# Attention with two routed layers: scaling q on ScalarE for every pair of heads, and one gate transpose a step

## The chip, the cores and the metric

The kernel runs on one core of a Trainium2 chip. A core has five engines that run their own instruction streams and wait for each other by semaphores: TensorE (PE, with its weight loads PEld), VectorE (DVE), ScalarE (ACT), GpSimd (POOL) and SyncE (SP), which in this kernel issues nearly all DMA transfers. The metric is the device time of one execution in microseconds (us); lower is better. Three runs of the kernel before took 1119.1 to 1124.27 us, with a median of 1122.33 us.

## The reference

Three parts run one after the other. Only the first and the entry of the second matter here.

```python
scores = scale * q @ k.T                      # 2 x 8 heads, 576 tokens, head size 64
bias = -(cum[:, :, :, None] - cum[:, :, None, :])          # cum: running sum of max(s, 0)
scores = where(causal, -1e9, scores + minimum(bias, 0))
attn = softmax(scores);  x = attn @ v         # x: 1152 tokens x 512
logits = x @ w_gate;  noisy = logits + log1p(exp(x @ w_noise)) * noise
top2 = the two largest of 8 experts per token # first routed layer (1024 hidden) ...
# ... then a second layer in which every expert sees every token, balanced 8 times
```

## The kernel before, in words

The 16 heads are taken in 8 pairs. Every number is carried as two halves of 16 bits (a high part and the rest), so that TensorE's products stay exact enough.

**Preparing a pair** (`nat_a`, `nat_d`, L130 to L149). q and k of a pair arrive as 32-bit tiles `stq` and `stk`. ScalarE writes 32*q as the high half (L135). Then q is scaled in place in 32 bits: by ScalarE for pairs 0 to 2 (L137), by GpSimd for pairs 3 to 7 (L139). ScalarE writes the high half of k (L140). At last VectorE forms the rest of k (L146) and GpSimd the rest of q (L148), which reads the scaled tile. `turn` (L189) turns the whole with a DMA transpose.

**Steps.** A loop over `it` from -4 to 16 is a software pipeline; I call its rounds step -4 to step 16. In step i TensorE makes the transposed scores of head i (L258, L260, L263), then the plain scores of head i+3 for their row maxima (L212, L215), a small turn of the maxima of the head before (L243), and the product with v of head i-1 (L350 to L354). ScalarE exponentiates (L267, L268), VectorE takes the maxima (L226), forms the rests `el` (L271), the negated maxima (L233, L235), and copies the operands of a later head (L203, L205). From step 13 on there are no plain scores, since no head is left. The maxima go by ScalarE (`rt`, L245) and a small DMA on SP (L246) into the rows 67 and 68 of `xq`; the product L260 of that head, two steps later, needs them.

**Beside the steps.** `between(it)` at the end of a step adds other work: from step 8 to 15 it writes 640 KB of zeros into the rows of one expert in memory (`xs_d<-z`, L661); from step 12 to 15 it loads one 512 KB piece of weights (`wst`, L536); in steps 13 and 14 it turns rows of `xall` (L703); and from step 9 on it advances the generator `route` for the first 512 tokens by one `yield` a step. In this order: weights, zeros, turns, route. The next pairs of heads are loaded after it (`stv`, L104, L106).

**route, first four tiles** (`pe` false). Four DMA transposes of the attention's output (L749, 256 KB each), then the gate's products on TensorE (L689, 48 of them), then logits `lg` on VectorE (L763), `na`, `ez`, `lu` on ScalarE (L767 to L771), some small VectorE and GpSimd work, and the choice of two experts. What set the order is the place of the `yield`s: each engine executes its instructions in the order in which the program was written, and SP's transfers all go through one queue (q1 of the page).

Of the kernel before, what the change touches and what calls it, by code (L numbers as in the profile page):

```python
# [12 lines left out]
AF = mybir.ActivationFunctionType  # L13
OP = mybir.AluOpType
# [3 lines left out]
def attention(tc, ctx, psum, q, k, v, s, xhl, scat, between, idle):  # L18
    nc = tc.nc
    B, H, S, D = q.shape  # L20
    G = B * H
    SQ = 32.0
# [26 lines left out]
    for i in range(NS):  # L49
        t = cst.tile([128, 2, 5, D], F32, name=f"stv{i}")  # L50
# [3 lines left out]
    for i in range(NX):  # L54
        t = cst.tile([128, 640], F16, name=f"xk{i}")
        xk.append(t)
        t = cst.tile([128, 640], F16, name=f"xq{i}")
        xq.append(t)
    for i in range(4):
        t = cst.tile([128, 2, 5, 130], F16, name=f"vx{i}")  # L60
        vxt.append(t)
    for i in range(3):
        t = cst.tile([128, 5], F32, name=f"mx{i}")
        mx.append(t)
        t = cst.tile([128, 10], F16, name=f"rn{i}")
        rn.append(t)
    for i in range(2):
        t = [cst.tile([128, 1664], F16, name=f"e{x}{i}") for x in "hl"]
# [58 lines left out]
    def nat(p):  # L127
        nat_a(p)
        nat_d(p)

    def nat_a(p):
        np_ = wk.tile([128, 2, 9, 128], F16, name="np_", bufs=3)
        nq, nk = np_[:, 0], np_[:, 1]
        qs, ks = ld.pop(("q", p)), ld.pop(("k", p))
        nc.scalar.activation(out=nq[:, :, 64:128], in_=qs, func=AF.Copy, scale=SQ)  # L135
        if p < 3:
            nc.scalar.activation(out=qs, in_=qs, func=AF.Copy, scale=SQ)  # L137
        else:
            nc.gpsimd.tensor_scalar(out=qs, in0=qs, scalar1=SQ, scalar2=None, op0=OP.mult)  # L139
        nc.scalar.activation(out=nk[:, :, 0:64], in_=ks, func=AF.Copy, scale=SQ)  # L140
        ld[p] = np_, qs, ks

# [273 lines left out]
    for it in range(-4, G + 1):  # L416
        p = (it + 5) // 2
# [46 lines left out]
def attention_moe_moe_kernel(  # L464
# [16 lines left out]
    nc = tc.nc  # L481
# [23 lines left out]
    def bank():  # L505
        return psum.tile([128, 512], F32, name="ps", tag="b")
# [162 lines left out]
    def xhl(t, n=None):  # L669

        return xhl_v[:, t] if n is None else xhl_v[:, t:t + n]
# [20 lines left out]
    def keep(ps, n, w):  # L692

        for _ in range(n):
            nc.tensor.matmul(out=ps[:, 0:w.shape[1]], lhsT=w[:, 0:128], rhs=w, start=True, stop=True)

    def turn2(c):

        todo = [(x, t) for x in range(2) for t in range(T2)]
        for i in range(0, 2 * T2, 4):  # L700
            ps = bank()
            for j, (x, t) in enumerate(todo[i:i + 4]):
                nc.tensor.matmul(out=ps[:, j * 128:(j + 1) * 128], lhsT=xhl(4 + t)[:, x, c * 128:(c + 1) * 128], rhs=ident,  # L703
                                 start=True, stop=True)
            for x in range(2):
                js = [(j, t) for j, (y, t) in enumerate(todo[i:i + 4]) if y == x]
                if js:
                    o = xt2[:, js[0][1]:js[-1][1] + 1, x * KD + c, :]
                    src = ps[:, js[0][0] * 128:(js[-1][0] + 1) * 128].rearrange("p (t n) -> p t n", n=128)
                    if c == 1:  # L710
                        idle.append(lambda o=o, src=src: nc.scalar.activation(out=o, in_=src, func=AF.Copy))
                    elif c < KD - 2:
                        idle.append(lambda o=o, src=src: nc.vector.tensor_copy(out=o, in_=src))
                    elif c == KD - 2 and i:
                        idle.append(lambda o=o, src=src: nc.vector.tensor_copy(out=o, in_=src))
                    elif c == KD - 2:
                        idle.append(lambda o=o, src=src: nc.scalar.activation(out=o, in_=src, func=AF.Copy))
                    elif x:
                        nc.vector.tensor_copy(out=o, in_=src)
                    else:  # L720
                        nc.scalar.activation(out=o, in_=src, func=AF.Copy)
# [9 lines left out]
    def route(r_p, t0, t1, pe):  # L731

        T = t1 - t0
        V = nc.vector

        def tmp(nm, *shape, dt=F32):
            return (r_p if pe or nm not in ("hot", "rk") else hx_p).tile([128, T] + list(shape), dt, name=nm)

        if pe:
            turn2(KD - 1)  # L740
            ps = bank()
            keep(ps, K2, iotac)
            for t in range(T):
                gate_mm(ps, t, xt2[:, t], wg, 16, (KD - 2, KD - 1))
        else:
            xts = []
            for t in range(t0, t1):
                xt = r_p.tile([128, 2 * KD, 128], F16, name="xt", bufs=T)
                nc.sync.dma_start_transpose(out=xt, in_=xhl(t).rearrange("p a d -> p (a d)"))  # L749
                xts.append(xt)  # L750
                if t - t0 in (1, 3):
                    yield
            yield
            ps = bank()
            for t in range(T):
                gate_mm(ps, t, xts[t], wg, 16)
        yield
        pg = ps[:, 0:T * 16].rearrange("p (t e) -> p t e", e=16)
        lg = tmp("lg", 16)
        if pe:  # L760
            V.scalar_tensor_tensor(out=lg, in0=pg, scalar=1.0 / (SX * SG), in1=pl, op0=OP.mult, op1=OP.add)
        else:
            V.tensor_scalar(out=lg, in0=pg, scalar1=1.0 / (SX * SG), scalar2=None, op0=OP.mult)  # L763
        if not pe:
            yield
        na = tmp("na", E)
        nc.scalar.activation(out=na, in_=lg[:, :, E:2 * E], func=AF.Abs)  # L767
        ez = tmp("ez", E)
        nc.scalar.activation(out=ez, in_=na, func=AF.Exp, scale=-1.0)
        lu = tmp("lu", E)  # L770
        nc.scalar.activation(out=lu, in_=ez, func=AF.Ln, bias=onec)  # L771
        u = tmp("u", E)
        if pe:
            yield
        V.tensor_scalar(out=u, in0=ez, scalar1=1.0, scalar2=None, op0=OP.add)
        d = tmp("d", E)
        if pe:
            yield
        V.scalar_tensor_tensor(out=d, in0=u, scalar=1.0, in1=ez, op0=OP.subtract, op1=OP.subtract)
        if pe:  # L780
            yield
        V.reciprocal(out=u, in_=u)
        if pe:
            yield
        V.tensor_tensor(out=d, in0=d, in1=u, op=OP.mult)
        V.scalar_tensor_tensor(out=d, in0=lg[:, :, E:2 * E], scalar=0.0, in1=d, op0=OP.max, op1=OP.subtract)
        yield
        for b, op in ((d, OP.add), (noise_sb[:, t0:t1, :], OP.mult), (lg[:, :, 0:E], OP.add)):
            (V if pe else nc.gpsimd).tensor_tensor(out=lu, in0=lu, in1=b, op=op)
        if not pe:  # L790
            yield
        for t in range(T):
            V.max(out=m8[:, t0 + t], in_=lu[:, t])
        for t in range(T):
            V.max_index(out=i8[:, t0 + t], in_max=m8[:, t0 + t], in_values=lu[:, t])
        hot = tmp("hot", 2, E)
        it = iota8.unsqueeze(1).unsqueeze(1).to_broadcast([128, T, 2, E])
        V.tensor_tensor(out=hot, in0=it, in1=i8[:, t0:t1, 0:2].unsqueeze(3).to_broadcast([128, T, 2, E]), op=OP.is_equal)
        V.tensor_tensor(out=mb[:, t0:t1, :], in0=hot[:, :, 0], in1=hot[:, :, 1], op=OP.add)
        if pe:  # L800
            ps = spare[0]
            for t in range(NT):
                nc.tensor.matmul(out=ps[:, NT * E:NT * E + E], lhsT=ones, rhs=mb[:, t, :], start=(t == 0), stop=(t == NT - 1))
            yield
        else:
            yield
            ps = bank()
        pr = ps[:, 0:T * E]
        nc.tensor.matmul(out=pr, lhsT=tri, rhs=mb[:, t0:t1, :].rearrange("p t e -> p (t e)"), start=True, stop=False)
        for sh in range(1, t1):  # L810
            a, b = max(t0, sh), t1
            nc.tensor.matmul(out=ps[:, (a - t0) * E:(b - t0) * E], lhsT=ones,
                             rhs=mb[:, a - sh:b - sh, :].rearrange("p t e -> p (t e)"), start=False, stop=(sh == t1 - 1))
        rk = tmp("rk", E)
        V.tensor_tensor(out=rk, in0=pr.rearrange("p (t e) -> p t e", e=E),
                        in1=base8.unsqueeze(1).to_broadcast([128, T, E]), op=OP.add)
        V.tensor_tensor(out=hot, in0=hot, in1=rk.unsqueeze(2).to_broadcast([128, T, 2, E]), op=OP.mult)
        sl = slot[:, t0:t1, :]
        V.tensor_reduce(out=sl, in_=hot, op=OP.add, axis=AX.X)
        V.tensor_copy(out=idx[:, t0:t1, :], in_=sl)  # L820
        if pe:
            yield
# [107 lines left out]
    with ExitStack() as m1:  # L930
# [84 lines left out]
        for e in range(E):  # L1015
# [33 lines left out]
            for b, n in BL:  # L1049
# [8 lines left out]
                else:  # L1058

                    for f in range(KF):  # L1060
# [5 lines left out]
                                                   op0=OP.mult, op1=OP.add)  # L1066
# [417 lines left out]
```

## Time and profile before

| | |
|---|---|
| profiled execution, its own time | 1117.76 us |
| its span from first to last instruction | 1116.0 us |
| runs: lowest, median, highest | 1119.1, 1122.33, 1124.27 us |
| PE busy | 1072.7 us (96%) |
| DVE, ACT, POOL busy | 599.3, 496.3, 230.4 us |
| mean granted clock of TensorE | 0.974 of full |

A page of the profile gives the busy time of each engine; the timeline of an engine gives start, duration, line, operation, and, in square brackets, how long it sat idle before and what ended that. A busy TensorE is not one that does much: the same products take longer at the lower of its two clocks (1.2 and 2.4 GHz), which the column PEclk shows as 0.50.

### The profile page before, as it was taken

To read this page: it belongs to the slowest core of one execution; us is meant where nothing else is said; L and a number is where in the kernel's file an instruction comes from. 1 tells how busy PE (TensorE), PEld (TensorE's weight loads), DVE (VectorE), ACT (ScalarE), POOL (GpSimd) and SP (SyncE) were. 2 spreads that over 40 slices of the span, in tenths; PEclk is the share of its full clock that TensorE was granted. 3 is DMA by queue.
4 is the path that set the end of the run, shared out by engine and by line. 5 is a ranking of instruction groups with operands and counts; after the bars stand their busy time and mean duration, and the time that the engine had idled before them with its cause. 6 is when DMAs were issued, how large, how long until landed. Compare 5 with 4: busy or idle time off the path is not lost.

```text
span 1116.0 us, 18342 instructions
## 1 busy us (share of the span) xinstructions
PE 1072.7 (96%) x7412; PEld 662.2 (59%) x7412; DVE 599.3 (54%) x1171; ACT 496.3 (44%) x928; POOL 230.4 (21%) x296
## 2 busy tenths in 40 slices
PE   7998899999999799999999999999999999999997
PEld 3565765555555385565666565566566566566554
DVE  8998685555554577553554543543453453454231
ACT  5786685555555243443433442442443442443220
POOL 6675352000004303521201301210210210220000
PEclk7798899999999899999999999999999999999999
DMA  5768769777756710120120121121121112020001
GB/s 98 134 116 149 201 245 300 191 228 212 210 167 207 245 49 3 56 76 27 51 76 20 57 62 34 38 76 38 38 77 38 37 59 57 20 58 1 11 29 50
DMA packets 131469, 107.14 MB, mean 96 GB/s; under 512 B 71504, under 2 KB 105600, under 8 KB 131376
## 3 DMA queue, kind: packets, MB, share of 16 engines
q1 hardware_dynamic: 127040, 91.86, 30.5%
q0 software_dynamic: 4336, 14.03, 3.6%
q8 instruction: 60, 0.98, 0.4%
q14 instruction: 33, 0.27, 0.1%
HBM read 79.03 MB, written 17.56 MB: 87 GB/s over the span
## 4 chain that ended last, share of the span: by engine, by line
PE 63%; issue 15%; POOL 4%; DMA 3%; DVE 2%; ACT 1%; POOLq 0%; DVEq 0%; SPq 0%; ACTq 0%
PE ps L1304 32%; PE ps L1250 25%; PE ps L1104 3%; POOL xs_d L828 2%; POOL yg L926 1%; DMA yg<-y_d,idy 1%; POOL y_d L1068 1%; DVE wp L560 0%; PE ps L1030 0%; DMA xsT<-xs_d 0%; PE ps L1031 0%; PE ps L1032 0%; DMA xs_d<-xall,idx 0%; DMA y_d<-y 0%; ACT wp L559 0%
## 5 line engine op out<-in xcount | busy, mean ns | idle before, releaser
L1304 PE MATMUL ps<-wp,hop 128*128 128x512 f16 x1536 | 366.6, 379 | 0.3 <-PE ps L1178 0.3
L1250 PEld LDWEIGHTS <-wp 128*128 128x128 f16 x2352 | 230.1, 98 | 101.1 <-issue 1.6
L1304 PEld LDWEIGHTS <-hop 128*128 128x128 f16 x1536 | 150.2, 98 | 141.8 <-issue 0.4
L560 DVE SCALAR_TENSOR_TENSOR wp<-wst,wp 128x1024 f16<-128x1024 f32 (+1 forms) x156 | 182.1, 1187 | 78.4 <-ACT wp L559 78.3
L1250 PE MATMUL ps<-xall,wp 128*128 128x256 f16 (+1 forms) x1344 | 192.1, 286 | 0.6 <-ACT z L1264 0.6
L559 ACT ACTIVATE wp<-wst 128x1024 f16<-128x1024 f32 (+1 forms) x156 | 153.8, 1009 | 22.7 <-DMA wst<-in_moe_w_dram 20.3
L1250 PE MATMUL ps<-xT,wp 128*128 128x256 f16 (+1 forms) x1008 | 150.9, 286 | 0.2 <-DVE z L1268 0.2
L570 POOL TENSOR_TENSOR wst<-wst 128x256 f32<-128x256 f32 x28 | 21.5, 767 | 441.1 <-DVE wp L560 441.1
L1268 DVE TENSOR_TENSOR z<-ps,z 128x256 f32<-128x256 f32 (+1 forms) x56 | 25.6, 457 | 137.6 <-ACT z L1267 137.6
L1285 DVE SCALAR_TENSOR_TENSOR acc<-ps,P,acc 128x512 f32<-128x512 f32 (+1 forms) x64 | 47.5, 742 | 94.6 <-PE ps L1304 94.6
L1273 DVE TENSOR_TENSOR z<-ps,z 128x256 f32<-128x256 f32 (+1 forms) x56 | 25.6, 458 | 111.8 <-PE ps L1250 111.8
L1030 PE MATMUL ps<-xsT,wp 128*128 128x320 f16 x256 | 77.3, 302 | 2.6 <-DMA xsT<-xs_d 2.6
L1221 ACT ACTIVATE hop<-z 128x1024 f16<-128x1024 f32 x56 | 59.1, 1056 | 46.2 <-DVE z L1273 46.2
L1031 PE MATMUL ps<-xsT,wp 128*128 128x320 f16 x256 | 77.3, 302 | 0.0
L1032 PE MATMUL ps<-xsT,wp 128*128 128x320 f16 x256 | 77.2, 302 | 0.0
L1222 DVE SCALAR_TENSOR_TENSOR hop<-z,hop 128x1024 f16<-128x1024 f32 x56 | 68.1, 1216 | 11.1 <-ACT hop L1221 11.1
L1264 ACT ACTIVATE z<-ps 128x256 f32<-128x256 f32 (+1 forms) x56 | 22.9, 410 | 108.2 <-PE ps L1250 108.2
L1271 ACT ACTIVATE z<-ps 128x256 f32<-128x256 f32 (+1 forms) x56 | 23.0, 410 | 99.8 <-PE ps L1250 99.8
L1267 ACT ACTIVATE z<-ps 128x256 f32<-128x256 f32 (+1 forms) x56 | 23.0, 410 | 96.3 <-PE ps L1250 96.3
L1104 PE MATMUL ps<-xall,wp 128*128 128x256 f16 (+1 forms) x384 | 49.7, 286 | 0.4 <-DVE xall L1095 0.4
L1056 PE MATMUL ps<-wp,hp 128*128 128x512 f16 x128 | 48.6, 379 | 1.5 <-DVE hp L1037 1.5
L1055 PE MATMUL ps<-wp,hp 128*128 128x512 f16 x128 | 48.5, 379 | 0.0
(273 smaller groups left out, 1497.8 us busy)
## 6 DMA issues: line engine op xcount, KB each, us to landing
wst<-in_moe_w_dram SPq DMA_DIRECT2D x100, 512.0 KB
wst<-in_moe_w_dram SPq DMA_DIRECT2D x56, 256.0 KB
xs_d<-z SPq DMA_DIRECT2D x8, 640.0 KB
y_d<-y POOLq DMA_DIRECT2D x14, 256.0 KB, 2.3
stq<-in_q_dram SPq DMA_DIRECT2D x8, 288.0 KB
stk<-in_k_dram SPq DMA_DIRECT2D x8, 288.0 KB
stv<-in_v_dram SPq DMA_DIRECT2D x16, 128.0 KB
out_dram<-acc SPq DMA_DIRECT2D x8, 256.0 KB
```

Source lines behind the costliest of these rows:

```text
L559: nc.scalar.activation(out=hi, in_=src, func=AF.Copy, scale=scale)
L560: run(todo, lambda: nc.vector.scalar_tensor_tensor(out=lo, in0=src, scalar=scale, in1=hi, op0=OP.mult, op1=OP.subtract))
L1030: nc.tensor.matmul(out=o, lhsT=wh, rhs=xt[:, c, :], start=(c == 0), stop=False)
L1031: nc.tensor.matmul(out=o, lhsT=wh, rhs=xt[:, KD + c, :], start=False, stop=False)
L1032: nc.tensor.matmul(out=o, lhsT=wl, rhs=xt[:, c, :], start=False, stop=(c == KD - 1))
L1055: nc.tensor.matmul(out=o, lhsT=hh[:, f, b:b + n], rhs=w2l[:, f, :], start=False, stop=False)
L1056: nc.tensor.matmul(out=o, lhsT=hp[:, f, lower_at(b):lower_at(b) + n], rhs=w2h[:, f, :], start=False, stop=(f == KF - 1))
L1104: nc.tensor.matmul(out=ps[:, s0:s1], lhsT=W[E, 0][u][:, c, f * 128:(f + 1) * 128], rhs=x2T[:, h * KD + c, c0 + s0:c0 + s1], start=(c + u + ...
L1221: nc.scalar.activation(out=hi, in_=x, func=AF.Relu)
L1222: nc.vector.scalar_tensor_tensor(out=lo, in0=x, scalar=0.0, in1=hi, op0=OP.max, op1=OP.subtract)
L1250: nc.tensor.matmul(out=o, lhsT=self.w[:, u, self.LEFT[m - 1], c * 128:(c + 1) * 128], rhs=x[h], start=start and c + u + h == 0, stop=c == ...
L1304: nc.tensor.matmul(out=ps, lhsT=x, rhs=w[h][:, f, d0:d0 + dn], start=(i + u + h == 0), stop=(i == KF - 1 and u == 1))
```

## The change

There are two edits. In `nat_a` the in-place scaling of q is now done by ScalarE for all pairs, so GpSimd's L139 is gone (five instructions) and ScalarE has five more. In `route` each of the four transposes is followed by its own `yield`, the `yield` behind the loop is gone, and so is the one between `lg` and `na`. The transposes, which stood two in step 9 and two in step 10, stand one each in steps 9 to 12; the gate's products move from step 12 to step 13, and `lg` from step 13 into step 14, together with `na`.

```diff
@@ nat_a
-        if p < 3:
-            nc.scalar.activation(out=qs, in_=qs, func=AF.Copy, scale=SQ)
-        else:
-            nc.gpsimd.tensor_scalar(out=qs, in0=qs, scalar1=SQ, scalar2=None, op0=OP.mult)
+        nc.scalar.activation(out=qs, in_=qs, func=AF.Copy, scale=SQ)
@@ route
                 xts.append(xt)
-                if t - t0 in (1, 3):
-                    yield
-            yield
+                yield
             ps = bank()
@@ route, behind lg
-        if not pe:
-            yield
         na = tmp("na", E)
```

SP's queue in steps 9 and 10 before: `xs_d<-z` are the zeros, `xt` the transposes, `stv` the rows of v, `xq_163` the maxima of head 12. Line numbers after the change are 3 lower here, and 7 lower behind `route`.

```order
L661 DMA xs_d<-z 640x1x512
L749 DMA_TRANSPOSE xt<-xall 128x8x128 x2
L104 DMA stv_152<-in_v_dram 128x4x64
L106 DMA stv_152<-in_v_dram 64x2x64
L246 DMA xq_163<-rt 2x5x128
L661 DMA xs_d<-z 640x1x512
L749 DMA_TRANSPOSE xt<-xall 128x8x128 x2
```

And after:

```order
L658 DMA xs_d<-z 640x1x512
L746 DMA_TRANSPOSE xt<-xall 128x8x128
L104 DMA stv_152<-in_v_dram 128x4x64
L106 DMA stv_152<-in_v_dram 64x2x64
L243 DMA xq_163<-rt 2x5x128
L658 DMA xs_d<-z 640x1x512
L746 DMA_TRANSPOSE xt<-xall 128x8x128
```

One transpose fewer stands ahead of the maxima of head 12.

SP's queue in steps 11 and 12 before (`wst` is the first piece of weights, `xq_167` belongs to head 14, `xq_169` to head 15):

```order
L661 DMA xs_d<-z 640x1x512
L104 DMA stv_153<-in_v_dram 128x4x64
L106 DMA stv_153<-in_v_dram 64x2x64
L246 DMA xq_167<-rt 2x5x128
L536 DMA wst<-in_moe_w_dram 128x1024
L661 DMA xs_d<-z 640x1x512
L246 DMA xq_169<-rt 2x5x128
```

And after:

```order
L658 DMA xs_d<-z 640x1x512
L746 DMA_TRANSPOSE xt<-xall 128x8x128
L104 DMA stv_153<-in_v_dram 128x4x64
L106 DMA stv_153<-in_v_dram 64x2x64
L243 DMA xq_167<-rt 2x5x128
L533 DMA wst<-in_moe_w_dram 128x1024
L658 DMA xs_d<-z 640x1x512
L746 DMA_TRANSPOSE xt<-xall 128x8x128
L243 DMA xq_169<-rt 2x5x128
```

The fourth transpose now stands behind the first weights and the zeros of step 12, and ahead of the maxima of head 15.

VectorE at the end of step 13 and in step 14 before (`x_2192` is the output of head 12, `x_2304` that of head 13):

```order
L367 TENSOR_TENSOR x_2192<-ps,dn 128x320
L271 TENSOR_TENSOR xall<-x_2045,xall 64x64
L763 TENSOR_SCALAR lg<-ps 128x64
L156 TENSOR_SCALAR vx_173<-stv_153 128x10x64
L157 SCALAR_TENSOR_TENSOR vx_173<-stv_153,vx_173 128x10x64
```

And after, in step 14:

```order
L360 TENSOR_SCALAR dn<-ps 128x5
L362 RECIPROCAL dn<-dn 128x5
L364 TENSOR_TENSOR x_2302<-ps,dn 128x320
L268 TENSOR_TENSOR xall<-x_2143,xall 64x64
L758 TENSOR_SCALAR lg<-ps 128x64
L768 TENSOR_SCALAR u<-ez 128x32
```

The logits moved behind the output of head 13, which waits for TensorE's product with v in step 14.

## Rows read from the trace of the kernel before

**Rows 1.** Page, part 4: the chain that ended last, by engine.
```profile
PE 63%; issue 15%; POOL 4%; DMA 3%; DVE 2%; ACT 1%; POOLq 0%; DVEq 0%; SPq 0%; ACTq 0%
```
**Rows 2.** Windows of the attention, with the line that names the columns.
```profile
core 0: us, PE busy (x) PEld busy (x) DVE busy (x) ACT busy (x) POOL busy (x), PEclk, DMA share, GB/s
44.00:84.00 40.00, 35.74 (x497) 25.25 (x496) 39.44 (x105) 33.65 (x80) 29.48 (x30) 0.96 0.72 124
102.00:104.60 2.60, 0.00 (x0) 0.00 (x0) 2.47 (x12) 0.10 (x1) 0.32 (x1) 1.00 0.72 155
104.60:121.80 17.20, 17.19 (x190) 11.96 (x190) 7.06 (x21) 9.64 (x24) 5.51 (x7) 0.50 0.87 192
```
**Rows 3.** Timeline of POOL, pair 7: start, duration, engine, line, operation, tiles.
```profile
84.19 1.65 POOL L139 TENSOR_SCALAR stq<-stq 128x576 f32<-128x576 f32 x1
85.92 1.42 POOL L148 TENSOR_TENSOR np__1551<-stq,np__1551 128x576 f16<-128x576 f32 x1
```
**Rows 4.** Timeline of DVE beside it.
```profile
84.69 0.33 DVE L203 COPY xk<-qkt 64x576 f16<-64x576 f16 x1
85.12 0.75 DVE L233 TENSOR_SCALAR rn<-mx 128x5 f16<-128x5 f32 x1
86.34 1.03 DVE L235 SCALAR_TENSOR_TENSOR rn<-mx,rn 128x5 f16<-128x5 f32 x1
87.69 0.74 DVE L146 SCALAR_TENSOR_TENSOR np__1551<-stk,np__1551 128x576 f16<-128x576 f32 x1
```
**Rows 5.** Groups of DVE by form, 32 to 88 us: count, busy us, mean ns.
```profile
L235 DVE SCALAR_TENSOR_TENSOR rn<-mx,rn 128x5 f16<-128x5 f32 x9 | 3.9, 430 | 0.0
L233 DVE TENSOR_SCALAR rn<-mx 128x5 f16<-128x5 f32 x9 | 2.9, 324 | 0.0
L146 DVE SCALAR_TENSOR_TENSOR np__780<-stk,np__780 128x576 f16<-128x576 f32 x1 | 1.8, 1827 | 0.0
L146 DVE SCALAR_TENSOR_TENSOR np__524<-stk,np__524 128x576 f16<-128x576 f32 x1 | 1.8, 1810 | 0.0
```
**Rows 6.** The same groups, 91 to 104 us, where no pair is prepared.
```profile
L233 DVE TENSOR_SCALAR rn<-mx 128x5 f16<-128x5 f32 x3 | 0.5, 172 | 0.0
L235 DVE SCALAR_TENSOR_TENSOR rn<-mx,rn 128x5 f16<-128x5 f32 x2 | 0.2, 124 | 0.0
```
**Rows 7.** Timeline of ACT, steps 8 and 9.
```profile
83.37 0.67 ACT L140 ACTIVATE np__1551<-stk 128x576 f16<-128x576 f32 x1
88.65 0.27 ACT L245 ACTIVATE rt<-ps 10x128 f16<-10x128 f32 x1 [0.79 <-PE ps L243]
```
**Rows 8.** Timeline of SP's DMA issues, steps 9, 10 and 12.
```profile
94.39 5.25 SPq L749 DMA_TRANSPOSE xt<-xall  x2
...
102.04 0.69 SPq L246 DMA_DIRECT2D xq<-rt  x1
...
114.46 0.40 SPq L536 DMA_DIRECT2D wst<-in_moe_w_dram  x1
```
**Rows 9.** Timeline of PE: starts of steps 12, 14 and 15, and the gate's products.
```profile
104.61 0.19 PE L260 MATMUL ps<-xq,xk 69*64 69x64 f16 x1 [2.83 <-DMA xq<-rt]
...
113.46 1.45 PE L689 MATMUL ps<-wg,xt 128*128 128x16 f16 x48
...
122.17 0.22 PE L258 MATMUL ps<-qkt 128*64 128x64 f16 x1
...
126.33 0.19 PE L258 MATMUL ps<-qkt 128*64 128x64 f16 x1
```
**Rows 10.** Windows of DMA: zeros alone, then weights and zeros of step 12.
```profile
104.00:108.00 4.00, 3.39 (x16) 1.75 (x15) 0.87 (x4) 3.47 (x8) 1.60 (x2) 0.59 0.88 173
115.00:120.00 5.00, 5.00 (x45) 3.25 (x45) 1.38 (x2) 3.85 (x10) 0.59 (x2) 0.50 0.98 269
```
**Rows 11.** Timeline of ACT: the gate's first three and the next exponentials.
```profile
127.02 0.23 ACT L767 ACTIVATE na<-lg 128x32 f32<-128x32 f32 x1
...
127.77 0.20 ACT L267 ACTIVATE eh<-ps 64x64 f16<-64x64 f32 x1
```
**Rows 12.** Timeline of DVE: the logits now, and the place that they move behind.
```profile
122.61 0.22 DVE L763 TENSOR_SCALAR lg<-ps 128x64 f32<-128x64 f32 x1
...
128.12 0.22 DVE L271 TENSOR_TENSOR xall<-x,xall 64x64 f16<-64x64 f32 x1
```

## The prediction, made blind

> **What bounds the kernel now.** I read the page's chain first [rows 1]: TensorE holds 63% of it, GpSimd 4%, transfers 3%, VectorE 2%. That is a mean over three parts, and the change lies in the first alone, so I went on to the windows [rows 2]. In the steps from 44 to 84 us VectorE is busy 39.44 of 40 us, TensorE 35.74, ScalarE 33.65, GpSimd 29.48: there VectorE sets the pace, and TensorE's gaps (4.26 of 40) are its covers. From 102 to 104.6 TensorE does nothing, and from 104.6 to 121.8 it is busy throughout, at granted clock 0.50, the level of 1.2 GHz. So two places matter: VectorE beside GpSimd up to 88 us, and the end of the attention, from 94 to 128 us, where the transposes and the gate stand. Then I read the timelines of both.
>
> **Edit 1, the scaling.** The timelines of GpSimd and VectorE side by side [rows 3, 4] show a coupling. L233 starts at 85.12 and ends at 85.87, while L139 ends at 85.84; L235 starts at 86.34 and ends at 87.37, while L148 ends at 87.34. Both small VectorE operations end 0.03 us behind the GpSimd operation that was running when they began. Where no pair is prepared they take 172 and 124 ns [rows 6]; over 32 to 88 us their means are 324 and 430 [rows 5]. The excess is 9 x (324 - 172) = 1.37 and 9 x (430 - 124) = 2.75 us. Two of the five L146 took 1.83 and 1.81 us [rows 5] against 0.74 [rows 4], another 2.16. Together 6.3 us of VectorE's time, where it is the bound.
>
> What is left after the edit is L148, 1.42 us [rows 3] for each of five pairs. It will start earlier: ScalarE has the scaled q ready in 0.67 us, the duration of L140 [rows 7], which has the same shape, and so L148 starts near 84.2 in pair 7, where L139 started. Some VectorE operation will begin inside it, and by chance at about its middle: a stall of about 0.75 a pair, 3.7 in five. Gain: 6.3 - 3.7 = 2.6 us. The ends: no stall at all, 6.3 gained; or L148 starts just ahead of a VectorE operation in all five pairs, 5 x 1.42 = 7.1 of stalls, 0.8 lost. I take 2.6, near the middle, since L148 falls at no fixed place against VectorE's order.
>
> Not everything is held: the copy L203 began at 84.69, inside L139, and took 0.33 us [rows 4]. The Trainium skill ("SBUF — State Buffer", on who interferes with whom) says that VectorE and GpSimd share a port pair exclusively and that who starts first keeps it for its whole instruction. The ends of L233 and L235 agree with it; L203, which ran inside L139, does not. By the rule every VectorE operation of that kind would wait, and the sum would go to the end of 0.8 lost.
>
> ScalarE gets 5 x 0.67 = 3.35 us more. It is busy 33.65 of 40 us [rows 2], and before its L245 it waits 0.79 us for TensorE [rows 7]: in a step there is cover of about this size, so I cost it at nothing. If the cover is gone, 3.35 us.
>
> **Edit 2, the first transpose pair taken apart.** In step 9 SP issues L749 twice at 94.39, which takes 5.25 us, and only then, behind v, the maxima of head 12, L246 at 102.04 [rows 8]. TensorE waits 2.83 us for just that transfer, until 104.61 [rows 9]. With one transpose fewer ahead, the transfer starts 5.25 / 2 = 2.6 us sooner, and of the wait about 0.3 is left: gain 2.5, between 0 (if something else in the queue holds it) and 2.83.
>
> More hangs on it. The clock is at 0.50 from this wait on [rows 2], and step 12 takes 113.46 - 104.61 = 8.85 us, step 13, from the gate's end at 113.46 + 1.45 = 114.91 to 122.17, takes 7.26; step 14, at the full clock, takes 126.33 - 122.17 = 4.16 [rows 9]. If the wait is gone and the clock stays up, step 12 takes about 8.85 x 4.16 / 7.26 = 5.1 and step 13 about 4.2, and TensorE comes to the gate's products, now behind step 13, at 104.61 - 2.5 + 5.1 + 4.2 = 111.4 instead of at the end of 122.17.
>
> **What is late next.** The fourth transpose is now behind the weights of step 12 and its zeros. SP issued those weights at 114.46 [rows 8]. The products cannot start before the transpose has landed. I count what the queue has to move from the zeros of step 9 on, which go out just ahead of 94.39: four times 640 KB of zeros, four transposes of 256 KB, 512 KB of weights, two parts of v of 160 KB, 4416 KB in all. Zeros move at 173 GB/s, weights and zeros together at 269 [rows 10]. So 1152 KB at 269 take 4.3 us, and 3264 KB at 173 take 18.9: 94.39 + 23.2 = 117.6. A transpose takes 2.6 us to issue instead of the 1.5 that its bytes need at 173, 1.1 more for the last: about 118.7, I take 119. Ends: 112, if all goes at 269 (16.4 us, and 1.1), and 122, about 16% slower than 173.
>
> TensorE then waits from 111.4 to 119, 7.6 us, and after such a wait the clock was low [rows 2]. The products take 1.1, between their 1.45 at the low clock [rows 9] and half of it. Step 14 starts at 120.1 instead of 122.17: 2.1 gained, between 4 and -1. If the clock is still low there, step 14 costs up to 7.26 - 4.16 = 3.1 more.
>
> The Trainium skill ("DMA: Bandwidth & Descriptors", on queues, rings and completion order) says that a DMA engine takes the descriptors of a ring in order. By it the small L246 of heads 14 and 15 waits behind zeros too; the wait of 2.83 us for L246 agrees. It speaks against the place of the fourth transpose.
>
> **The logits in step 14.** `lg` took 0.22 us at 122.61 and is now behind L271, which ran at 128.12 [rows 12]. On ScalarE `na` ran at 127.02, ahead of the exponentials of the next head at 127.77 [rows 11]. It now waits for `lg`: 128.12 + 0.22 + 0.22 = 128.56, 1.5 us later, and the exponentials and step 15's products with them stand behind it. If TensorE at the low clock is late anyway, the two waits are one. Bounds: 0, since other work of step 15 can go on, to 1.6 beside a slow step. I take 1.7 for the two together, between 0 and 4.7.
>
> **Sum.** Edit 1 gains 2.6; the start of step 14 gains 2.1; the end of step 14 loses 1.7: 3.0 us. The profiled execution took 1117.76 us, 4.57 below the median of 1122.33 and below the lowest of the runs, 1119.1; its span is 1116.0, with 1.8 around it. So 1117.76 becomes 1114.8, and on the median's scale 1122.33 - 3.0 = **1119.3**.
>
> **Rivals.**
> *A, the transpose is in time (much faster).* The queue moves everything at 269 GB/s and the transpose lands at 112, when TensorE comes at 111.4; with 0.7 for the products step 14 starts at 112.7, 9.5 before 122.17. Less 1.5 for `na`, and with 2.6 of edit 1: 10.6 gained, 1111.7. For it: the second of the windows [rows 10]. Against: that one had weights in it, and zeros alone went at 173.
> *B, no change.* GpSimd's L148 holds VectorE as long as L139 and L148 did together, since it starts at L139's place, and the wait before the gate takes all that the shorter wait before step 12 gave: 1122. For it: L148's 1.42 us is nearly as long as L139's 1.65 [rows 3]. This is also the case in which the change doesn't do what it is said to do: VectorE is held as before.
> *C, slower.* The gate's products wait for the fourth transpose past 121, the point from which step 14 starts later than before. Landing at 122, with 1.1 of products, step 14 starts at 123.2, 1.0 late; the clock, down in the wait, stays low through step 14, 3.1 more; edit 1 gives nothing: 4.1 lost, 1126.5. For it: transposes, zeros and weights of four steps in one queue [rows 8], and the DMA share of 0.98 in the window with weights [rows 10], which leaves no reserve. Against: with TensorE ahead of its old time, SP issues earlier than 114.46, too.
>
> **How the numbers follow.** The forecast 0.45 (its own range 1116.8 to 1121.3), A 0.17, B 0.20, C 0.18. I leave out the outer part of A and of C, about 0.2 together: 1111 to 1127. A measurement of this kernel can tell about 0.5% from no change, 5.6 us. Faster by more than that are A and the outer 0.07 of the forecast, 0.24; slower by more are the worst half of C, 0.08 (a second low stretch of the clock, with `na`'s 1.6 on top); within it 0.68.
>
> **What would show it.** Edit 1: VectorE's small operations beside L148 (now L145) last 0.75 us on the mean, their sum of excess over 32 to 88 us falls from 6.3 to near 3.7, and pair 7's L143 starts about 0.5 us earlier a pair. Edit 2: L243, the maxima of head 12, goes out at about 99.5 instead of 102.04, the gap before step 12 is under 1 us, and the granted clock stays at 1.00 from 104 to 111. Gate: an idle time of about 7 us before the first of the 48 products, ended by the transfer of a transpose, and a low clock behind it. `na` waits for VectorE's `lg`. I am wrong if the granted clock is low without a wait before step 12 (then step 14 starts near 122 all the same, and B holds), if another transfer ahead of L243 keeps it at 102, or if the time is beyond either end because steps 14 and 15 lose more than 4.7.

## The result and the profile after

The changed kernel took 1129.04 us (median of 12 runs, 1124.23 to 1135.21), the kernel before 1122.01 in the same comparison; the ratio is 1.0063, 95% interval 1.0041 to 1.0085: about 7 us slower. I had forecast 1119.3, 3 us faster. The profiled execution of the changed kernel took 1133.08 us, near the upper end of its runs, while that of before lay near the lower end of its own; so I don't explain the 15 us between the two traces, but the 7 us between the medians, and I check the main readings on the traces of other kernels.

The chain of waits by engine [rows 1] shows little here, since the loss sits in some 30 us of 1131. Windows of the changed kernel (us, then busy time of each engine, the granted clock, the DMA share and GB/s), answering to [rows 2]:

```profile
core 0: us, PE busy (x) PEld busy (x) DVE busy (x) ACT busy (x) POOL busy (x), PEclk, DMA share, GB/s
106.00:116.60 10.60, 9.74 (x149) 7.07 (x148) 10.25 (x32) 9.01 (x23) 4.59 (x8) 1.00 0.90 182
...
117.74:125.81 8.07, 0.00 (x1) 0.01 (x1) 1.36 (x2) 0.00 (x0) 0.49 (x1) 0.77 0.96 192
...
126.20:132.30 6.10, 6.10 (x66) 4.53 (x63) 2.88 (x6) 4.11 (x10) 1.50 (x3) 0.50 0.94 312
```

Steps 12 and 13 now run at the full clock (row 106 to 116.6), as forecast. Then TensorE stands still for 8.07 us, and step 14 runs at 0.50, 1.2 GHz. The timeline of TensorE, with the gate's products and the starts of steps 14 and 15, beside [rows 9]:

```profile
116.61 1.13 PE L686 MATMUL ps<-wg,xt 128*128 128x16 f16 x36
125.81 0.49 PE L686 MATMUL ps<-wg,xt 128*128 128x16 f16 x12 [8.07 <-DMA xt<-xall]
126.23 0.26 PE L255 MATMUL ps<-qkt 128*64 128x64 f16 x1
...
133.00 0.22 PE L255 MATMUL ps<-qkt 128*64 128x64 f16 x1
```

The products of the first three tiles run at once (36 instructions); the last 12 wait for the fourth transpose. Step 14 takes 133.00 - 126.23 = 6.77 us, before it took 4.16. SP's timeline of the same steps, beside [rows 8]:

```profile
97.06 0.61 SPq L658 DMA_DIRECT2D xs_d<-z  x1
97.78 2.97 SPq L746 DMA_TRANSPOSE xt<-xall  x1
...
104.57 3.48 SPq L746 DMA_TRANSPOSE xt<-xall  x1
108.10 1.46 SPq L104 DMA_DIRECT2D stv<-in_v_dram  x1
...
111.07 3.45 SPq L746 DMA_TRANSPOSE xt<-xall  x1
...
116.62 0.69 SPq L243 DMA_DIRECT2D xq<-rt  x1
117.35 0.39 SPq L533 DMA_DIRECT2D wst<-in_moe_w_dram  x1
117.80 0.61 SPq L658 DMA_DIRECT2D xs_d<-z  x1
118.45 4.96 SPq L746 DMA_TRANSPOSE xt<-xall  x1
```

A single transpose behind zeros holds SP for 3 to 5 us; the pair before took 5.25. The fourth goes out at 118.45 and is read by TensorE at 125.81. VectorE's `lg` and ScalarE's `na`, beside [rows 11, 12]:

```profile
133.69 0.22 DVE L758 TENSOR_SCALAR lg<-ps 128x64 f32<-128x64 f32 x1
...
133.95 0.23 ACT L760 ACTIVATE na<-lg 128x32 f32<-128x32 f32 x1 [2.28 <-DVE lg L758]
```

### The profile page after: what moved, and what is told of

The parts are those of the page before. It is cut to its first block, busy times and chain, and to the rows that moved or that the text cites. A ratio compares the mean times of both kernels' runs of the same rounds, so it can differ in the third digit from the quotient of the medians.

```text
span 1131.2 us, 18348 instructions
## 1 busy us (share of the span) xinstructions
PE 1078.1 (95%) x7412; PEld 664.7 (59%) x7412; DVE 599.1 (53%) x1171; ACT 499.6 (44%) x933; POOL 220.9 (20%) x291
## 4 chain that ended last, share of the span: by engine, by line
PE 65%; issue 18%; DVE 7%; POOL 4%; DMA 3%; ACT 2%; SPq 0%; POOLq 0%; DVEq 0%; ACTq 0%
PE ps L1297 32%; PE ps L1243 25%; PE ps L1097 3%; POOL xs_d L821 2%; DVE mx L223 2%; POOL yg L919 1%; PE ps L209 1%; POOL y_d L1061 1%; DMA yg<-y_d,idy 1%; PE ps L255 1%; DVE el L268 1%; PE ps L257 1%; DMA xt<-xall 1%; DVE xk L200 1%; DMA y_d<-y 1%
## 5 line engine op out<-in xcount | busy, mean ns | idle before, releaser
L1023 PE MATMUL ps<-xsT,wp 128*128 128x320 f16 x256 | 76.5, 299 | 2.6 <-DMA xsT<-xs_d 2.6
L1024 PE MATMUL ps<-xsT,wp 128*128 128x320 f16 x256 | 76.5, 299 | 0.1
L1025 PE MATMUL ps<-xsT,wp 128*128 128x320 f16 x256 | 76.5, 299 | 0.0
```

The lines of the kernel that those rows point to most:

```text
L1023: nc.tensor.matmul(out=o, lhsT=wh, rhs=xt[:, c, :], start=(c == 0), stop=False)
L1024: nc.tensor.matmul(out=o, lhsT=wh, rhs=xt[:, KD + c, :], start=False, stop=False)
L1025: nc.tensor.matmul(out=o, lhsT=wl, rhs=xt[:, c, :], start=False, stop=(c == KD - 1))
```

## The experiments

Each was timed in five rounds beside the kernel before; the ratio is to that, with its 95% interval. For comparison: the changed kernel has 1.0063 (1.0041 to 1.0085). Where I subtract two ratios they come from different comparisons, so both intervals count. The first question was which edit costs the time. Theory Q: the fourth transpose, late in SP's queue, and the low clock behind it. Rival S: the scaling, since the changed kernel's TensorE was 3.1 us late at 93 us already.

**The scaling alone.**

```diff
-        if p < 3:
-            nc.scalar.activation(out=qs, in_=qs, func=AF.Copy, scale=SQ)
-        else:
-            nc.gpsimd.tensor_scalar(out=qs, in0=qs, scalar1=SQ, scalar2=None, op0=OP.mult)
+        nc.scalar.activation(out=qs, in_=qs, func=AF.Copy, scale=SQ)
```

> Kernel before with the scaling of q on ScalarE for all pairs, route as before. Theory Q (the loss is all in the gate: its wait of 8.07 us for the fourth transpose and the low clock behind it): this one is 0 to 3 us faster than before (about 1120), and step 14 starts at or before 122. Rival S (the loss comes from the scaling: TensorE was 3.1 us late at 93 us already, since the first low stretch of the clock ended at 50.4 us instead of 39.9): this one is 3 us or more slower than before (1125 and up), and its low stretch ends near 50 as well.

Measured: 0.9986 (0.9963 to 1.0008). The scaling doesn't cost the time, and its first low stretch of the clock (granted clock 0.50) ended at 42.1 us, not near 50; S falls. What it does to VectorE is seen in the groups by form from 32 to 88 us (count | busy us, mean ns | idle before). The copy of before, which [rows 5] don't have:

```profile
L203 DVE COPY xk<-qkt 64x576 f16<-64x576 f16 x9 | 4.1, 457 | 0.0
```

And with the scaling on ScalarE:

```profile
L200 DVE COPY xk<-qkt 64x576 f16<-64x576 f16 x9 | 6.4, 715 | 0.0
...
L232 DVE SCALAR_TENSOR_TENSOR rn<-mx,rn 128x5 f16<-128x5 f32 x9 | 2.1, 231 | 0.0
L230 DVE TENSOR_SCALAR rn<-mx 128x5 f16<-128x5 f32 x9 | 1.9, 208 | 0.0
...
L143 DVE SCALAR_TENSOR_TENSOR np__524<-stk,np__524 128x576 f16<-128x576 f32 x1 | 0.8, 759 | 0.0
```

L235 fell from 430 to 231 ns, L233 from 324 to 208, and no L146 takes 1.8 us any more; but the copy rose from 457 to 715 ns, 9 x 258 = 2.3 us. Of this 1.7 us lie in two copies that begin inside GpSimd's L145, which now starts earlier in its step. They take 1.01 and 1.27 us and end about 0.15 us behind it; in the kernel before the same two began inside L139 and took 0.29 each, as long as one beside no GpSimd operation. The first of them:

```profile
60.05 1.28 POOL L145 TENSOR_TENSOR np__1036<-stq,np__1036 128x576 f16<-128x576 f32 x1 [0.50 <-ACT stq L136]
...
60.48 1.01 DVE L200 COPY xk<-qkt 64x576 f16<-64x576 f16 x1
```

The other 0.6 us lie in copies beside other GpSimd operations (L159, L268 and a memset).

**The route alone.** The kernel before with the second edit of the change only.

> Kernel before with the new route alone, q still scaled by GpSimd for pairs 3 to 7. Theory Q: nearly all of the loss is here, 1128 to 1130, a gate wait of 5 us or more ended by a transpose, and a low clock behind it. Rival S: within 2 us of before, with the first low stretch ending near 40.

Measured: 1.0056 (1.0032 to 1.0081), nearly all of the change's 1.0063. Timeline of TensorE, its gate and the starts of steps 14 and 15:

```profile
122.19 0.49 PE L689 MATMUL ps<-wg,xt 128*128 128x16 f16 x12 [7.06 <-DMA xt<-xall]
122.61 0.26 PE L258 MATMUL ps<-qkt 128*64 128x64 f16 x1
...
129.77 0.22 PE L258 MATMUL ps<-qkt 128*64 128x64 f16 x1
```

The wait is 7.06 us, and step 14 then takes 7.16 instead of 4.16. Step 14 starts at 122.61, within half a us of the 122.17 of before: in this trace the late start isn't the loss, the slow step is most of it.

**The fourth transpose in step 11.** The changed kernel with the third and the fourth together:

```diff
                 xts.append(xt)
-                yield
+                if t - t0 != 2:
+                    yield
+            yield
```

> The changed kernel, but the fourth transpose is issued in step 11 with the third, ahead of the weights and zeros of step 12 (1152 KB, 4.3 us); gate products and logits stay where the change put them. Theory Q: the gate's wait falls from 8.07 us to 2 to 4, and the time falls by 4 to 5 us, to 1124 to 1125. Rival S: the wait falls but the time stays within 2 us of the changed kernel.

Measured: 0.9987 (0.9964 to 1.001). More than I expected: 0.0076 off the changed kernel, some 8.5 us. The gate's 48 products run in one piece, and step 14 takes 4.36 us:

```profile
117.30 1.35 PE L686 MATMUL ps<-wg,xt 128*128 128x16 f16 x48
118.58 0.22 PE L255 MATMUL ps<-qkt 128*64 128x64 f16 x1
...
122.94 0.22 PE L255 MATMUL ps<-qkt 128*64 128x64 f16 x1
```

I had left 2 to 4 us of wait, and none was left; with it went the slow step 14. Part of that is TensorE's own lateness: it came to the gate 22.4 us behind the zeros of step 9 (94.95 to 117.30), in the changed kernel 19.6. In steps 12 and 13 it was slow, since it had waited for the maxima of head 12, although one transpose fewer stood ahead of them than before:

```profile
105.07 0.19 PE L257 MATMUL ps<-xq,xk 69*64 69x64 f16 x1 [2.00 <-DMA xq<-rt]
```

**The gate later, the transposes as before.** The kernel before with the gate's products behind step 13 and `lg` and `na` in step 14:

```diff
                 if t - t0 in (1, 3):
                     yield
             yield
+            yield
...
-        if not pe:
-            yield
         na = tmp("na", E)
```

> Kernel before with its transposes two in step 9 and two in step 10, but the gate's products behind step 13 and the logits in step 14, as the change has them; scaling as before. Theory Q (the place of the transposes does the harm): same as before within 2 us, no wait at the gate, and the wait of 2.8 us for the maxima of head 12 is there. Rival G (the later gate does the harm, by logits and na in step 14): 3 us or more slower than before with no wait at the products.

Measured: 1.0001 (0.9979 to 1.0024). The later gate and `na` behind `lg` cost nothing that can be told (at most 2.7 us, by the interval): the products wait for nothing, and step 14 takes 129.16 - 124.80 = 4.36 us.

```profile
123.52 1.35 PE L689 MATMUL ps<-wg,xt 128*128 128x16 f16 x48
124.80 0.22 PE L258 MATMUL ps<-qkt 128*64 128x64 f16 x1
...
129.16 0.22 PE L258 MATMUL ps<-qkt 128*64 128x64 f16 x1
```

The next three ask what delays the fourth transpose, and whether the low clock is a cost of its own.

**Transposes ahead of weights and zeros.** The changed kernel, with `route` advanced first in steps 9 to 12:

```diff
+            if it == 9:
+                first.append(route(r_p, 0, 4, False))
+            if 9 <= it <= 12:
+                next(first[0], None)
             if 12 <= it < 16:
                 w_load(0, it - 11)
             if 8 <= it < 8 + E:
                 zero_rows(it - 8, z)
-            if it == 9:
-                first.append(route(r_p, 0, 4, False))
...
-            if it >= 9:
+            if it > 12:
                 next(first[0], None)
```

> The changed kernel, but in steps 9 to 12 the transpose of the step is issued ahead of that step's weights and zeros; nothing else is moved, and the fourth transpose stays in step 12. Theory Q (what counts is what stands ahead of the fourth transpose in the queue): 1152 KB less ahead of it, at 269 GB/s 4.3 us, so a gate wait of about 8.07 - 4.3 - 1 (two issues) = 3, and 4 to 8 us less time than the changed kernel, 1113 to 1118 on the scale of the last runs (before 1117, changed 1124). Rival P (the place in step 12 is too late in itself, since SP reaches it only when the maxima of head 14 are ready): the wait stays over 5 us and the time within 2 us of the changed kernel's.

Measured: 0.998 (0.9956 to 1.0005), 0.0083 or 9.3 us under the changed kernel. The fourth transpose stands in the same step and at the same yield; P falls. SP's timeline, the first and the fourth transpose:

```profile
94.85 1.25 SPq L746 DMA_TRANSPOSE xt<-xall  x1
...
111.42 1.28 SPq L746 DMA_TRANSPOSE xt<-xall  x1
```

They hold SP for 1.25 and 1.28 us (all four 1.25 to 1.52) instead of 2.97 to 4.96, and the fourth is out at 111.42 instead of 118.45. The gate, now in one piece:

```profile
115.09 1.35 PE L686 MATMUL ps<-wg,xt 128*128 128x16 f16 x48
116.37 0.22 PE L255 MATMUL ps<-qkt 128*64 128x64 f16 x1
...
120.73 0.22 PE L255 MATMUL ps<-qkt 128*64 128x64 f16 x1
```

**Zeros in steps 1 to 8.** The changed kernel with `if 1 <= it < 1 + E: zero_rows(it - 1, z)`.

> The changed kernel with the zeros written in steps 1 to 8 instead of 8 to 15, so that of the queue's 4416 KB from step 9 to the fourth transpose 2560 are gone. Theory Q: no wait at the gate, or under 1 us, gate products at about 110 to 113 and step 14 right behind them: 6 to 12 us less than the changed kernel, 1112 to 1118 on the scale of the last runs. Rival T (SP's issue of a transpose, 3 to 5 us each, is what takes the time, whatever moves): the wait stays at 4 us or more. Rival E (the zeros disturb the loads of the pairs in the early steps): no wait at the gate, but step 9 starts 3 us or more later.

Measured: 1.0114 (1.0074 to 1.0153), slower than the change itself. The transposes hold SP for 1.25 to 2.01 us here too, which speaks against T, but rival E came true, and more than I had put: in the early steps the zeros stand ahead of the maxima of the heads. The waits of TensorE from 44 to 108 us (sum, times, longest), and the start of step 10:

```profile
PE ps L257 <- DMA xq<-rt: 10.3, 4, 5.1
```

```profile
105.86 0.22 PE L255 MATMUL ps<-qkt 128*64 128x64 f16 x1
```

So the run says nothing about the gate: its place is reached 11 us late.

**A busy wait.** The changed kernel, with products of no use in the wait:

```diff
             for t in range(T):
+                if t == T - 1:
+                    for _ in range(48):
+                        nc.tensor.matmul(out=ps[:, 64:384], lhsT=iotac[:, 0:128], rhs=iotac, start=True, stop=True)
                 gate_mm(ps, t, xts[t], wg, 16)
```

> The changed kernel with 48 products of 320 columns more on TensorE, of no use, ahead of the products of the fourth tile: about 6.5 us of work inside the wait of 8.07. Theory K (the low clock behind the wait is a cost of its own, beside the wait): the granted clock stays at 1.00 through the gate, steps 14 and 15 take 4 to 4.5 us instead of 6.8, and the time is 3 to 6 us lower than the changed kernel's, 1118 to 1121 on the scale of the last runs. Rival N (only the wait costs, the low clock comes anyway or hides behind VectorE): the same time as the changed kernel within 2 us.

Measured: 1.0021 (1.0001 to 1.0041), 0.0042 or 4.7 us under the changed kernel (with the two intervals taken together, 1.4 to 8). Timeline of TensorE and windows:

```profile
116.29 1.13 PE L686 MATMUL ps<-wg,xt 128*128 128x16 f16 x36
117.28 6.68 PE L753 MATMUL ps<-iotac 128*128 128x320 f16 x48
124.89 0.46 PE L686 MATMUL ps<-wg,xt 128*128 128x16 f16 x12 [0.93 <-DMA xt<-xall]
125.28 0.22 PE L255 MATMUL ps<-qkt 128*64 128x64 f16 x1
...
129.64 0.22 PE L255 MATMUL ps<-qkt 128*64 128x64 f16 x1
```

```profile
116.30:125.00 8.70, 7.77 (x91) 5.68 (x89) 2.27 (x4) 0.50 (x2) 1.62 (x2) 1.00 0.92 197
125.30:129.60 4.30, 4.22 (x74) 3.34 (x72) 2.18 (x5) 3.60 (x9) 0.37 (x2) 1.00 0.95 308
```

The transpose comes no sooner (124.89), but the clock stays at 1.00 and step 14 takes 4.36 us. Work without use in the wait wins back a part of the loss, by the middle value more than half: theory K holds. The time alone would just leave room for rival N, which allowed 2 us; the trace doesn't, with step 14 at 4.36 us instead of 6.77.

**The fourth alone ahead.** As the kernel with all four ahead, but in step 12 only (`if it == 12:` in the place of `9 <= it <= 12`).

> The changed kernel, but in step 12 alone the transpose is issued ahead of the weights and zeros; the first three stay behind the zeros of their steps. Theory W (the 1152 KB of step 12 are the harm): the gate's wait falls from 8.07 to 3 us or less, and the ratio to before is 0.996 to 1.001, most of what the order of all four gave (0.998). Rival I (the three others count as much, since behind zeros each holds SP for 3.0 to 3.5 us and ahead of them 1.25 to 1.5): the wait stays at 4 us or more, and the ratio at 1.002 or above.

Measured: 0.9996 (0.9978 to 1.0013). SP and the gate:

```profile
113.43 3.05 SPq L746 DMA_TRANSPOSE xt<-xall  x1
...
118.77 0.68 SPq L243 DMA_DIRECT2D xq<-rt  x1
119.49 1.56 SPq L746 DMA_TRANSPOSE xt<-xall  x1
```

```profile
121.52 1.05 PE L686 MATMUL ps<-wg,xt 128*128 128x16 f16 x36
122.92 0.46 PE L686 MATMUL ps<-wg,xt 128*128 128x16 f16 x12 [0.35 <-DMA xt<-xall]
```

The third, still behind zeros, takes 3.05; the fourth 1.56, and the gate waits 0.35 us. TensorE came to the gate 4.9 us later here than in the changed kernel's trace (121.52 against 116.61), which shortens the wait too; so I count from SP's L243 just ahead of the weights. From there to the last twelve products it is 122.92 - 118.77 = 4.15 us, in the changed kernel 125.81 - 116.62 = 9.19. So 5.0 of the 7.7 us by which the wait is shorter come from the order, near the 4.3 that I had for 1152 KB. The other 2.7 come from TensorE's lateness: it had waited 2.48 us for the maxima of head 12 and was slow behind that. Theory W holds for most of the loss; what the three others add is within the intervals.

**Which version is best.** Two more that use this: the new scaling, transposes ahead of the zeros, and the gate's products behind step 12 as before; once with two transposes each in steps 9 and 10, once with one in step 9, one in 10, two in 11.

> Kernel before with the new scaling, and its transposes two in step 9 and two in step 10 ahead of the zeros of these steps; gate products behind step 12, logits in 13, na in 14 as before. If one transpose a step is worth nothing once they stand ahead of the zeros: ratio to before 0.996 to 1.000, as the changed kernel with its transposes ahead (0.998), and no wait over 1 us before step 12. If the pair still holds the maxima of head 12: a wait of 2 to 3 us there, the low clock behind it, and a ratio of 0.999 or above.

> As the last, but one transpose in step 9, one in 10 and two in 11, each ahead of the zeros of its step; gate products behind step 12. It should have neither the wait of 2.8 us for the maxima of head 12 nor a wait at the gate: ratio 0.994 to 0.999. If the last two land too late for products behind step 12, a gate wait of 2 us or more and a ratio of 0.999 or above.

Measured: 0.9972 (0.9952 to 0.9991) and 0.9974 (0.9954 to 0.9995). Both beat the kernel before in this comparison, and equally; one transpose a step is worth nothing of its own that could be told. In the first, the wait before step 12 is down from 2.83 to 0.92 us with two transposes in step 9, and the pair holds SP for 2.63 us instead of 5.25 (a wait of 0.97 for the maxima of head 13 follows):

```profile
103.59 0.19 PE L257 MATMUL ps<-xq,xk 69*64 69x64 f16 x1 [0.92 <-DMA xq<-rt]
```

**What the scaling gives there.** The pairs ahead of the zeros with the old scaling, and with the new one again, on one chip:

> Kernel before, with nothing changed but the transposes of steps 9 and 10 issued ahead of the zeros; q scaled by GpSimd for pairs 3 to 7 as before. If the gain of the pairs ahead of the zeros (ratio 0.9972) comes from their order alone: 0.996 to 0.999. If the new scaling gives half of it or more: 0.9985 to 1.001.

> The kernel with both the new scaling and the pairs of transposes ahead of the zeros, once more beside the last one, on the same chip: 0.995 to 0.999 if the first result (0.9972) holds. If the scaling is worth anything here, this is 0.001 or more below the last.

Measured: 0.9984 (0.9958 to 1.0009) and 0.9981 (0.9956 to 1.0007). The ratios differ by 0.0003, the medians (1120.14 and 1117.21) by 2.9 us; with intervals of about 2.8 us either way, what the scaling gives can't be told. The repeat's interval reaches past 1. So the gain of the order is best put at 0.2 to 0.3%: the intervals of the first two kernels are clear of 1, those of these two are not.

## Why the prediction was wrong, step by step

**The transpose's landing: the step that failed.** I put it at 118.7, 24.3 us behind 94.39, which is the issue of the first transposes. The zeros of step 9 went out at 93.68, so it was 25.0 us behind them:

```profile
93.68 0.61 SPq L661 DMA_DIRECT2D xs_d<-z  x1
```

It took from 97.06 to 125.81 = 28.75 in the changed kernel, and in the route alone 27.71 (zeros issued at 94.48, products at 122.19). The windows of the changed kernel, then of the route alone:

```profile
97.06:125.81 28.75, 19.82 (x312) 14.64 (x309) 20.43 (x57) 14.92 (x39) 9.30 (x12) 0.88 0.92 167
```

```profile
94.48:122.19 27.71, 19.93 (x314) 14.89 (x311) 20.44 (x58) 15.06 (x40) 9.38 (x12) 0.89 0.89 173
115.13:122.19 7.06, 0.00 (x1) 0.01 (x1) 1.41 (x2) 0.00 (x0) 0.38 (x1) 0.80 1.00 214
```

Both sides of the sum were off, the bytes too few and the rate too high. The bytes: at 167 and 173 GB/s these stretches moved 4.8 MB each, and I had counted 4416 KB as 4.42 MB. I had left out the 128 KB of v that go out in step 10 (108.10 in SP's timeline above) and had taken a KB as 1000 bytes, where the tiles have 1024; the rest is small transfers and what was still under way. The rate: I had counted 173 and 269 by [rows 10], 182 together, by which 4.8 MB would take 26.4 us. But the last part, the weights and zeros, did not move at 269: the wait at the gate shows 192 in the changed kernel and 214 in the route alone. Why it was less than in the window with 269 stays open. Rival C's landing at 122, 27.6 us behind 94.39, came nearest, but by a slower rate for the same count of bytes, so in part by luck.

That the 1152 KB of step 12 decide is shown by the fourth transpose moved alone (5.0 us less from SP's L243 to the products, ratio 0.9996); that it is not the step in which it stands, by all four ahead.

**The low clock behind the wait: mis-sized.** I put 1.7 us for step 14 and `na` together. Step 14 took 6.77 us in the changed kernel, 7.16 in the route alone, against 4.16: 2.6 to 3.0 more for it, near my upper bound of 3.1. Both traces show a second low stretch after it, at granted clock 0.50 (136.4 to 143.2 us in the route alone, 139.2 to 149.4 in the changed kernel), which I had put at a chance of 0.08. The busy wait had one as well (138.8 to 145.6), and so had the kernel with the fourth transpose in step 11 (131.0 to 137.8), in which TensorE did not wait at the gate at all; so not all of it is the gate's. The busy wait measures the clock's part: 4.7 us of the 7, between 1.4 and 8. The start of step 14, where I had counted 2.1 gained, gained nothing: in the route alone TensorE is 0.4 us later than before at step 14 (122.61 against 122.17), 3.4 at step 15 (129.77 against 126.33), and 4.4 at the first product of the expert layer (157.07 against 152.69); its span ends 4.6 later (1120.6 against 1116.0). In this trace nearly all of the loss arises behind the wait, since the wait itself is paid by what steps 12 and 13 gained.

**Edit 2, the first pair: right in the issue, too large in the gain.** Without a second transpose ahead, the maxima of head 12 go out 6.0 us behind the zeros of step 9 (97.06 to 103.08 in the changed kernel), before 8.4 (93.68 to 102.04): 2.3 sooner, where I had 2.6. But the transfer then took longer: from its issue to TensorE's product 3.9 us (103.08 to 107.02), before 2.57. So the product came only 1.0 us sooner behind those zeros, and 0.8 to 1.0 in the three other traces with this queue in which TensorE waited; in the route alone, where nothing waited, at least 1.8. I had set the whole 2.6 against the wait. Whether TensorE waits depends on when it comes, too. It waited 0.81 us in the changed kernel, 0.87 in the busy wait and not at all in the route alone, but 2.00 with the fourth transpose in step 11 and 2.48 with the fourth alone ahead, which have the same queue up to there. In the first three a low stretch of the clock, at 0.50, stood just ahead (98.3 to 101.5 us in the changed kernel, 95.5 to 98.8 in the route alone), and TensorE came to step 12 8.8 to 9.1 us behind the zeros of step 9, in the last two 7.9 and 7.3. So that the wait went away is in part luck.

In the route alone steps 12 and 13 ran at 1.00. From the start of step 12 at 103.60 to the products at 114.07 they took 10.5 us with the turns, where I had 9.3; before, 8.85 and 7.26 and the wait of 2.83, 18.9 together. In this trace the gain of 8.4 us went into the wait at the gate, 7.06, and the products' own place behind it.

**`na` behind `lg`: no cost that can be told.** The changed kernel shows the wait that I described, 2.28 us for `lg`, but the gate later without late transposes measured 1.0001, with a wait of 1.62 us of the same kind in its trace. My lower bound of 0 was the right one: TensorE's step 15 goes on meanwhile.

**Edit 1: the sum nearly right, the mechanism in part; the gain in time not shown.** VectorE's time for the same instructions from 32 to 88 us fell by 2.2 us (I had 2.6): 4.9 less in L233, L235 and L146, 2.3 more in the copy L203, 0.4 more in L229. I had left 3.7 us of stalls with the small operations; 1.3 are left with them, and it is the copies that now wait. I had read the copy's 0.33 us inside L139 as a sign that copies are not held. The two that began inside L145 took 1.01 and 1.27 us, so the operation of VectorE alone doesn't tell held from unheld. The Trainium skill ("SBUF — State Buffer", on who interferes with whom) says that a VectorE copy can take the pair of ports shared with GpSimd, so that one of the two waits. The two copies inside L145 agree; the three inside L139 (0.29, 0.29 and 0.33 us, the last in [rows 4]) show no wait.

A sign that I had named did not come: pair 7's L143 started at 88.51 us with the scaling alone, 0.8 later than before (87.69), in a trace whose first low stretch ended 2.2 us later. The time moved by a ratio of 0.9986, from 4.2 us gained to 0.9 lost, and the direct comparison gives 0.9984 against 0.9981 by the ratios and 2.9 us by the medians. So 2.6 us is neither confirmed nor excluded.

**The early 3.1 us.** In the changed kernel's trace the first low stretch of the clock ended at 50.4 us; before it was 39.9. Eight other traces are of kernels with the same instructions up to step 8; the stretch ended at 41.3 to 42.2 us in six of them, at 50.1 in the busy wait and at 60.0 with the fourth alone ahead. It varies among kernels that are the same there, so the change alone doesn't bring it. Whether the new scaling makes a late end likelier isn't shown: in the four traces with the old scaling it ended at 39.9 to 41.1. It may be why the profiled run lay 4 us above the median.

**The chances.** I gave the slower side 0.08, though rival C's mechanism had 0.18, by pricing it at 4.1 us. It was the case that came, at 7. Rivals A and B did not come: the queue moved at 167 to 173 GB/s up to the landing, and VectorE's stalls did become shorter.

What stays open: why the second low stretch, behind step 15, comes in some traces and not in others (the kernel before, the scaling alone, the later gate and all four ahead have none), and so how much of the 7 us it carries on the mean.

## What to carry to other kernels

Count what stands ahead of a transfer in its queue, and place what another engine waits for ahead of bulk work that nobody waits for; putting transposes ahead of such work in the same steps gave 7.5 us (the fourth alone) to 9.3 (all four). Issuing a transfer sooner is not landing it sooner by as much: 2.3 us in the queue were 0.8 to 1.0 at TensorE in four traces. A wait that was removed in one place is worth only what the next wait leaves: in the route alone 8.4 us gained in steps 12 and 13 were spent at the gate. Price a long idle time of TensorE with the slow step behind it, and not only by the idle time.

## What the runs showed of the hardware

A transpose of 256 KB issued behind 640 KB of zeros holds SP itself, not only the queue: one took 2.97 to 4.96 us of SP behind zeros (the longest also behind 512 KB of weights) and 1.25 to 1.56 ahead of them. The same VectorE copy took 0.29 to 0.33 us in the three cases in which it began inside GpSimd's L139, and 1.01 and 1.27 in the two in which it began inside L145. Filling TensorE's wait with 6.68 us of products without use kept the granted clock at 1.00 through the gate and step 14 and made the kernel 4.7 us faster (1.4 to 8).
